# Graph message passing: one adding scatter for three steps, into a store that is zeroed ahead

## The chip, the cores and the metric

One core of one Trainium2 chip runs the whole kernel in one launch. The metric is the device time of the launch in microseconds (us); lower is better. The core has a matrix engine (PE; its weight loads are listed as PEld), a vector engine (DVE), a scalar engine (ACT), a general engine (POOL, which here issues the indirect transfers) and SyncE (SP, which here issues plain transfers). Each runs its own list of instructions in order; semaphores hold an instruction until others are done.

## The reference

```python
# N = 12500 nodes, E = 800000 edges, D = 64, 16 edge features
def reference(x, e_attr, src, dst, w_msg, w_upd):
    m_in = jnp.concatenate([x[src], x[dst], e_attr], axis=-1)
    msg = _silu(m_in @ w_msg)                          # one message of 64 an edge
    agg = _segment_sum(msg, dst, N)                    # summed at its target node
    return _silu(jnp.concatenate([x, agg], axis=-1) @ w_upd)
```

All is float32; `src` and `dst` are drawn at random.

## The kernel before

**Buckets.** The nodes are cut into 128 buckets of 98. An edge belongs to the bucket of its target. The kernel sorts the edges' records (16 features and one number that holds the source and the place in the bucket, 17 floats, `R`) by bucket into a store `st` in DRAM. Each bucket owns a stretch of it, and a pointer (`ptr`) says where its next record goes. At the same time it takes full tiles of 128 records of one bucket from the store and computes the messages and their sums.

**Steps.** The edges come as 6250 tiles of 128, in 782 *steps* of 8 tiles (`M`). A step runs through three periods: `onehot` and `sums` (ACT and DVE: which edge is in which bucket, and running counts); `count`, `ranks` and `expand` (PE sums give each edge its rank within its bucket in this *chunk*, and DVE writes its record into the slot of that rank, array `X`); `move` (PE multiplies the one-hot `hf` with `X` and so gathers, for each of 128 buckets, a row of slots in the PSUM tile `pl`). A chunk is several tiles whose products add up in one `pl`. The slots grow with the tiles (`LIM`: 13 for the first two tiles, then 17, 21, 24, 27, 30), so later tiles of a chunk have wider products. The first 140 chunks (`N8`) are *plain* ones of 8 tiles, one a step; then come 428 of 12 tiles (`C`), two in three steps. Such a triple of steps has three turns: turn 0 holds tiles 0 to 7 of its first chunk, turn 1 the last four of the first and the first four of the second, turn 2 tiles 4 to 11 of the second.

At a chunk's end ACT copies `pl` to `blk`, `Chunk.place` (DVE) makes the next pointer from the counts, and `Chunk.scatter` (POOL) writes the 128 rows to the store at the pointers that held before this chunk. A row is written with all its slots; the unused ones behind a bucket's end are overwritten by the next chunk. A chunk in which a bucket's slots do not suffice is noted in `LOST` and done again at the end.

**Groups and batches.** The kernel forms a *group* of 48, 24 or 64 tiles of the store (units of one, two, then four tiles) as soon as a plan made with random draws (`Draws`) is sure that they are full. SP loads them (`rt<-st`), and they are worked off in *batches* of 8 tiles (6 in the second kind): POOL gathers the sources' rows, one indirect transfer a tile (`g<-A_d`, L649); PE transposes (`tq`, L668) and multiplies (`pre`, L677), DVE adds, ACT applies silu, and PE sums per node (`ag`, L698), which DVE adds to `ACC` (L710). The gathers go into four buffers in turn; the first gather of a batch waits for the sum of the batch four before.

**Order.** `period()` writes the order out by hand: the new batch's first four gathers, then the scatter of the chunk that ended in the period before, then the other gathers; `onehot`; the group's small operations; `count`; the transposes; the sum `ag`; `ranks`; the message; `sums` and `expand`; `move`; `product`; and `place`. Each engine's list follows it. The steps end after 785 periods; periods with batches alone follow, then the last tiles of each bucket and the update of the nodes.

Of the kernel before, what the change touches and what calls it, by code (L numbers as in the profile page):

```python
# [24 lines left out]
N8 = 140  # L25
# [4 lines left out]
XR = 2 + W  # L30
# [14 lines left out]
SUMMED = "the sum that this reads waits for the gathers into its buffer, the older ones there were read ahead of them"  # L45
LISTED = "the work list holds buckets and tiles of the store"


def mpnn_kernel(tc, x, e_attr, src, dst, w_msg, w_upd, out):
# [7 lines left out]
    CAPT = (K8 * S8 + (NCH - K8) * S) // P + 2  # L57
# [3 lines left out]
    NREC = TOP * P  # L61
# [11 lines left out]
    with es:  # L73
# [11 lines left out]
        A_d = dr.tile([NB * BK, D], F32, name="A_d")  # L85
        XU_d = dr.tile([BK, NBK * D], F32, name="XU_d")
        st = dr.tile([NREC, R], F32, name="st")
        st_t = st.rearrange("(t e) c -> t (e c)", e=P)

# [34 lines left out]
        ioS = cb[:, BK:BK + S]  # L124
        hit = cb[:, P:P + M * S].rearrange("p (k s) -> p k s", s=S)
# [3 lines left out]
        nc.vector.tensor_scalar(out=ioS, in0=iof[:, 0:S], scalar1=RK, scalar2=None, op0=OP.add)  # L129

# [8 lines left out]
        nc.vector.tensor_scalar(out=ub[1], in0=ipf, scalar1=float(CAPT), scalar2=None, op0=OP.mult)  # L139
# [5 lines left out]
        capm = cp.tile([NBK, 2 + len(FIRST)], F32, name="capm")  # L145
# [191 lines left out]
        ACCf = ACC.rearrange("p b k -> p (b k)")  # L337
        for t in X:
            nc.gpsimd.memset(t[:, :, 0:1], 1.0)
        nc.gpsimd.memset(sent, 0.0)  # L340
# [6 lines left out]
        def later():  # L347
# [5 lines left out]
            if len(zeros) == 15:  # L353
                for k in range(P // SR):
                    nc.sync.dma_start(st_t[D0:D0 + DUM, k * SR * R:(k + 1) * SR * R], sent[0:DUM].rearrange("p a b -> p (a b)"))
            elif len(zeros) == 13:
                nc.sync.dma_start(BW[BK:KQ], w_msg[2 * D:2 * D + DE, None, :].to_broadcast([DE, NBK, D]))
# [4 lines left out]
        bp = pool("bp", 2)  # L362
# [8 lines left out]
        state = dict(x=0, rt=0, u=1, ptr=ptr0, done=done0, stage=0, taken=0, straight=True)  # L371

        blocks = []
        gathers = []
# [4 lines left out]
        class Step:  # L379


            def __init__(c, hi, rec, index, n=M):

                c.hi, c.rec, c.n = hi, rec, n
# [4 lines left out]

                c.last = {k: K8 + (index * M + k) // c.size for k in range(n) if c.pos[k] == c.size - 1}  # L390
# [44 lines left out]
            def expand(c, rs=None):  # L435
# [6 lines left out]
                nc.vector.tensor_tensor(out=c.x[:, :, 1], in0=rank, in1=limc[:, c.turn, :], op=OP.is_ge)  # L442
                nc.vector.tensor_tensor(out=hit, in0=ioS[:, None, :].to_broadcast([P, M, S]), in1=rank[:, :, None].to_broadcast([P, M, S]), op=OP.is_equal)
                for k in range(0, c.n, 2):
                    n = LIM[c.pos[k]]
                    nc.vector.tensor_tensor(out=c.x[:, k:k + 2, 2:2 + n * R].rearrange("p k (s c) -> p k s c", c=R), in0=hit[:, k:k + 2, 0:n, None].to_broadcast([P, 2, n, R]),  # L446
                                            in1=c.rec[:, k:k + 2, None, :].to_broadcast([P, 2, n, R]), op=OP.mult)

            def move(c, part=None):
# [4 lines left out]
                for k in reversed(range(c.n)) if whole else range(c.n):  # L454
# [6 lines left out]
                    w = 2 + LIM[n] * R  # L461
                    ends = n == (0 if whole else c.size - 1)
                    nc.tensor.matmul(pl[:, 0:w], c.hf[:, k, :], c.x[:, k, 0:w], start=(n == (c.size - 1 if whole else 0)), stop=ends, skip_group_check=True)  # L463
                    if ends:
                        w = 2 + LIM[c.size - 1] * R
                        end = Chunk(*c.last.values())
                        end.blk = bp.tile([NBK, XR], F32, name="blk")[:, 0:w]
                        nc.scalar.activation(end.blk, pl[:, 0:w], AF.Copy)  # L468
                return end

        class Chunk:


            def __init__(c, index):
                c.index, c.m = index, M if index < K8 else min(C, NT - K8 * M - (index - K8) * C)

            def place(c, ptr_new):

                c.ptr, b = state["ptr"], c.blk
                lost = LOST[:, c.index:c.index + 1]  # L480
                nc.vector.scalar_tensor_tensor(out=lost, in0=b[:, 1:2], scalar=0.0, in1=b[:, 0:1], op0=OP.is_gt, op1=OP.mult)
                nc.vector.scalar_tensor_tensor(out=ptr_new, in0=b[:, 0:1], scalar=lost, in1=c.ptr, op0=OP.subtract, op1=OP.add)
                state["ptr"] = ptr_new

            def scatter(c):
                i = nc.gpsimd.indirect_dma_start(out=st, out_offset=bass.IndirectOffsetOnAxis(ap=c.ptr, axis=0), in_=c.blk[:, 2:], in_offset=None)  # L486
                tc.declare_no_dep(i.ins, group="units", reason=WHOLE)
                blocks.append(i.ins)
# [4 lines left out]
        class Group:  # L493


            def __init__(g, u, ptr, done_old, done_new, ceil, gt=GT, base=None, cap=None, bt=BT):
# [4 lines left out]
                g.quick = cap is not None  # L501
                g.nl = NL[u]
# [32 lines left out]
            def fourth(g):  # L535
                k = g.k
                gu = g.gu
                if k == 0:
                    urec = g.u * P
                    c = (urec - 1) / (2.0 * urec) * (1.0 if g.ceil else -1.0)  # L540
# [8 lines left out]
                    nc.vector.scalar_tensor_tensor(out=new, in0=v, scalar=-MAGIC, in1=g.done_old, op0=OP.add, op1=OP.subtract)  # L549
                    nc.vector.tensor_tensor(out=t1, in0=g.base, in1=g.done_old, op=OP.add)  # L550
# [164 lines left out]
        def period(step=None, batch=None, ptr_new=None):  # L715
# [49 lines left out]
            if p:  # L765
                p.move(1)
            if e:
# [10 lines left out]
        class Draws:  # L778
# [21 lines left out]
            def free(d, u):  # L800
# [3 lines left out]
                return [[min((c - o * P) // r, k) - n for c, o, n, k in zip(*v, caps)] for v in zip(d.cnt, d.base, d.done)]  # L804
# [65 lines left out]
        def step():  # L870
# [5 lines left out]
            if pipe["z"] and pipe["z"].last:  # L876
# [310 lines left out]
```

## Time and profile before

| what | value |
|---|---|
| time, median of 3 runs | 10877.64 us (10877.01 to 10887.08) |
| span of the profiled execution | 10886.0 us (the longest of the three times is 10887.08) |
| busy: PE, DVE, POOL, ACT | 82%, 66%, 60%, 47% of the span |
| granted PE clock, mean | 0.885 |
| `g<-A_d` gathers on POOL | 6322, 949 ns each |
| `st<-blk` scatters on POOL | 568, about 1000 ns each |
| HBM read, written | 330.05 MB, 152.30 MB |

Line numbers (L649) are those of the kernel before. In a row of a timeline the first number is the start in us, the second the duration, then engine, line, operation, what it writes and reads (`out<-in`), and in brackets how long the engine was idle before it and what ended that. In a table of groups the busy time and the mean duration in ns of one follow the count, and then the idle time before them with its releasers ("issue": nothing that the profile shows; "remote": a semaphore whose release is matched to no instruction).

### The profile page before, as it was taken

How to read it: one execution, taken by the hardware profiler on the slowest of the kernel's cores; microseconds unless marked ns; L12 is line 12 of the kernel's file. 1: busy time of each engine (PE TensorE's matmuls, PEld its weight loads, DVE VectorE, ACT ScalarE, POOL GpSimd, SP SyncE). 2: the span in 40 equal slices, each digit the busy share in tenths (PEclk: the TensorE clock that was granted, in tenths of full speed). 3: DMA queues.
4: the chain of work that ended last, by engine and by line, in shares of the span. 5: the costliest groups of instructions: out<-in, count | busy, mean ns of one | idle time of the engine just before them, and what ended most of it. 6: DMA issues, size and time to landing. Idle time of an engine off the chain costs nothing. (4 is left out here: it accounts for less than half of the span.)

```text
span 10886.0 us, 155616 instructions
## 1 busy us (share of the span) xinstructions
PE 8949.9 (82%) x49053; PEld 6219.2 (57%) x49816; DVE 7231.4 (66%) x15936; ACT 5082.6 (47%) x12594; POOL 6571.4 (60%) x6908
## 2 busy tenths in 40 slices
PE   8788888888888888888888888888888888888556
PEld 5566655555555555555555555555555555555555
DVE  7777776666666666766666666666666666766232
ACT  6455554444444444444444444444444444544211
POOL 2565666666666666666666666666666666666555
PEclk9999998999989988999998999999899998988555
DMA  3111111111111111111111111111111111111212
GB/s 97 44 49 48 49 49 46 43 47 42 47 42 46 45 44 45 44 43 44 46 43 46 44 44 43 46 47 43 45 42 46 43 47 44 44 45 41 46 36 44
DMA packets 662903, 501.15 MB, mean 46 GB/s; under 512 B 492983, under 2 KB 529911, under 8 KB 662071
## 3 DMA queue, kind: packets, MB, share of 16 engines
q0 software_dynamic: 238976, 349.72, 12.3%
q1 hardware_dynamic: 422775, 141.27, 5.9%
q8 instruction: 400, 6.55, 0.3%
q14 instruction: 432, 3.54, 0.1%
q10 hardware_dynamic: 320, 0.07, 0.0%
HBM read 330.05 MB, written 152.30 MB: 44 GB/s over the span
## 5 line engine op out<-in xcount | busy, mean ns | idle before, releaser
L649 POOL DMA_INDIRECT g<-A_d,sidx x6322 | 5997.6, 949 | 3658.7 <-issue 1620.7
L463 PE MATMUL pl<-X,hf 128*128 128x291 f32 (+5 forms) x12512 | 4745.0, 524 | 476.4 <-issue 428.3
L463 PEld LDWEIGHTS pl<-X,hf 128*128 128x128 f32 x12512 | 2538.7, 211 | 2159.4 <-issue 1737.4
L446 DVE TENSOR_TENSOR X<-cb,rec 128x442 f32<-128x442 f32 (+5 forms) x3128 | 2646.6, 908 | 26.7
L396 ACT ACTIVATE hf<-iof,shi 128x128 f32<-128x128 f32 x6256 | 1908.8, 389 | 1360.4 <-PE pl L463 449.0
L671 ACT ACTIVATE qt<-tq 114x1024 f32<-114x1024 f32 (+1 forms) x818 | 811.7, 992 | 2951.3 <-remote 2298.5
L433 DVE TENSOR_REDUCE rank<-z 128x8 f32<-128x1024 f32 x782 | 954.5, 1221 | 1270.3 <-remote 874.9
L677 PEld LDWEIGHTS pre<-w,qt 114*128 114x128 f32 x10496 | 1392.5, 209 | 687.8 <-ACT qt L671 467.1
L677 PE MATMUL pre<-w,qt 114*128 114x64 f32 x10496 | 1395.2, 291 | 345.6 <-ACT qt L671 317.6
L710 DVE TENSOR_TENSOR ACC<-ag,ACC 64x98 f32 x1938 | 496.7, 256 | 1553.3 <-remote 1131.7
L698 PE MATMUL ag<-q,g 128*64 128x98 f32 x12644 | 882.3, 276 | 490.4 <-remote 236.2
L698 PEld LDWEIGHTS ag<-q,g 128*64 128x64 f32 x12644 | 681.6, 151 | 668.8 <-issue 381.7
L668 PE MATMUL tq<-ident,q 128*114 128x128 f32 x6322 | 929.9, 294 | 103.3 <-issue 91.5
L668 PEld LDWEIGHTS tq<-ident,q 128*114 128x114 f32 x6322 | 812.6, 147 | 238.7 <-issue 122.6
L397 ACT ACTIVATE hf<-hf,ones 128x1024 f32<-128x1024 f32 x782 | 898.8, 1149 | 25.4
L486 POOL DMA_INDIRECT st<-blk,ptrs x567 | 567.2, 1000 | 561.4 <-ACT blk L468 272.2
L659 DVE TENSOR_TENSOR q<-cb,lo 128x784 f32<-128x784 f32 (+1 forms) x818 | 768.7, 940 | 96.1 <-PE ag L698 46.3
L468 ACT ACTIVATE blk<-pl 128x512 f32<-128x512 f32 (+1 forms) x568 | 324.9, 572 | 818.2 <-PE pl L463 500.9
L426 PE MATMUL z<-G,onesb 128*128 128x384 bf16 x1564 | 529.8, 339 | 78.9 <-issue 25.2
L682 ACT ACTIVATE g<-g 128x512 f32<-128x512 f32 (+1 forms) x818 | 498.4, 609 | 192.5 <-DVE g L681 111.8
L681 DVE TENSOR_TENSOR g<-pre,g 128x512 f32<-128x512 f32 (+1 forms) x818 | 541.3, 662 | 51.4 <-issue 37.2
L677 PE MATMUL pre<-BW,qt 114*128 (+1 forms) x2148 | 326.3, 314 | 99.0 <-ACT qt L671 64.8
(138 smaller groups left out, 5243.9 us busy)
## 6 DMA issues: line engine op xcount, KB each, us to landing
g<-A_d,sidx POOLq DMA_INDIRECT x6322
ea<-in_e_attr SPq DMA_DIRECT2D x260, 192.0 KB
rt<-st SPq DMA_DIRECT2D x1312, 34.0 KB
st<-blk,ptrs POOLq DMA_INDIRECT x567
rt<-st SPq DMA_DIRECT2D x434, 8.5 KB
nodes<-in_x SPq DMA_DIRECT2D x62, 98.0 KB
ACC<-rt SPq DMA_DIRECT2D x11, 544.0 KB
rt<-st SPq DMA_DIRECT2D x320, 17.0 KB
```

The source lines that it names most:

```text
L396: nc.scalar.activation(c.hf[:, k, :], iof, AF.Square, bias=c.hi[:, k:k + 1])
L397: nc.scalar.activation(c.hf, c.hf, AF.Relu, bias=ones, scale=-1.0)
L433: nc.vector.tensor_reduce(out=c.rank, in_=c.z, axis=AX.X, op=OP.max)
L446: nc.vector.tensor_tensor(out=c.x[:, k:k + 2, 2:2 + n * R].rearrange("p k (s c) -> p k s c", c=R), in0=hit[:, k:k + 2, 0:n, None].to_broad ...
L463: nc.tensor.matmul(pl[:, 0:w], c.hf[:, k, :], c.x[:, k, 0:w], start=(n == (c.size - 1 if whole else 0)), stop=ends, skip_group_check=True)
L486: i = nc.gpsimd.indirect_dma_start(out=st, out_offset=bass.IndirectOffsetOnAxis(ap=c.ptr, axis=0), in_=c.blk[:, 2:], in_offset=None)
L649: j = nc.gpsimd.indirect_dma_start(out=t.g[:, i, :], out_offset=None, in_=A_d, in_offset=bass.IndirectOffsetOnAxis(ap=t.grp.sidx[:, k:k + ...
L659: nc.vector.tensor_tensor(out=t.q[:, 0:n, 0:BK], in0=ioB[:, None, :].to_broadcast([P, n, BK]), in1=t.grp.lo[:, i0:i0 + n, None].to_broadca ...
L668: nc.tensor.transpose(t.tq[0:KQ, j * P:(j + 1) * P], t.q[:, j, :], ident)
L671: nc.scalar.activation(t.qt[:, 0:w], t.tq[0:KQ, 0:w], AF.Copy)
L677: nc.tensor.matmul(t.pre[:, i * D:(i + 1) * D], t.qt[:, i * P:(i + 1) * P], w, start=True, stop=True)
L698: o = nc.tensor.matmul(t.ag[t.half(v), v // 2 * BK:(v // 2 + 1) * BK], t.g[:, i, :], t.q[:, i, 0:BK], start=(k == 0), stop=(k == u - 1))
```

## The change

Two consecutive 12-tile chunks, that is three steps, now make one row of 60 slots (`ROW`) and one scatter. In the first chunk of the pair the ranks run downwards from slot 29, in the second upwards from slot 30, so that each bucket's records of both lie side by side around the middle. The row is written at the old pointer + the first chunk's count − 30. Since it then begins with unused slots over records that are there already, the scatter adds (`compute_op=OP.add`) instead of writing, and the store must hold zeros: 265 pieces of 128 × 60 records, copied by SP from a zero tensor `Z_d` in DRAM, four pieces ahead (`LEAD`). If either chunk of a pair has a bucket that overflows, that bucket's row goes to a place aside. `blk` becomes one buffer `BLK` with two halves, and the counts are copied apart (`cnt`). `place` runs once a pair and makes the pair's own address (`to`) as well as the next pointer. Groups formed from step 38 on may only take units that end 30 records below the pointer (`back`). The plain chunks at the beginning are 53 instead of 140, so there are 53 plain chunks and 243 pairs.

```diff
-N8 = 140
+N8 = 53
...
-XR = 2 + W
+XR = 2 + W + 2
+ROW = 2 * S
+LEAD = 4
...
+    REACH = [S8 * (i + 1) for i in range(K8)] + [S8 * K8 + ROW * (i + 1) for i in range(NPR)]
+    PIECES = [(r + S + ROW - 1) // ROW for r in REACH]
...
+        ioD = cp.tile([P, 2, S], F32, name="ioD")
+        nc.vector.tensor_scalar(out=ioD[:, 0, :], in0=iof[:, 0:S], scalar1=-1.0, scalar2=RK + S - 1, op0=OP.mult, op1=OP.add)
+        nc.vector.tensor_copy(ioD[:, 1, :], ioS)
...
+        BLK = lp.tile([NBK, 2, W], F32, name="BLK")
...
             if len(zeros) == 15:
+                nc.sync.dma_start(Z_d, z[:, 0:ROW * R])
+                nc.sync.dma_start(st[ASIDE:NREC, :].rearrange("(b r) c -> b (r c)", b=NBK), z[:, 0:ROW * R])
...
+        def fill():
+            a = (P - S + len(filled) * ROW) * R
+            z = nc.sync.dma_start(st_b[:, a:a + ROW * R], Z_d)
+            tc.declare_no_dep(z.ins, group="blocks", reason=AHEAD)
+            tc.add_to_no_dep_group("zeros", z.ins)
+            filled.append(z.ins)
...
             def expand(c, rs=None):
...
-                nc.vector.tensor_tensor(out=c.x[:, :, 1], in0=rank, in1=limc[:, c.turn, :], op=OP.is_ge)
+                for a, b in ((0, C - M), (C - M, M)) if turn else ((0, M),):
+                    f = 1 if c.right[a] else 3 + W
+                    nc.vector.tensor_tensor(out=c.x[:, a:b, f], in0=rank[:, a:b], in1=lim[:, a:b], op=OP.is_ge)
...
+                    h = 0 if c.right[k] else S - n
+                    a = 2 + h * R
...
             def move(c, part=None):
...
-                    w = 2 + LIM[n] * R
+                    w = LIM[n] * R
+                    a, b, o = (0, 2 + w, 0) if c.right[k] else (2 + W - w, 4 + W, 2)
...
+            def keep(c, pl, right):
+                if c.single or c.side == 0:
+                    prior["cnt"] = sm.tile([NBK, 8], F32, name="cnt")
...
+                if c.main:
+                    nc.scalar.activation(c.cnt[:, c.side, :], pl[:, f:f + 2], AF.Copy)
+                c.blk = BLK[:, c.side, 0:n]
+                nc.scalar.activation(c.blk, pl[:, a:a + n], AF.Copy)
...
             def place(c, ptr_new):
...
+                    both, at, whole, to = [c.all[:, k:k + 1] for k in range(4, 8)]
+                    n, lost = c.cnt[:, :, 0], c.cnt[:, :, 1]
+                    c.ptr = to.bitcast(I32)
+                    nc.vector.tensor_scalar(out=whole, in0=lost[:, 0:1], scalar1=lost[:, 1:2], scalar2=0.0, op0=OP.add, op1=OP.is_equal)
+                    nc.vector.tensor_scalar(out=at, in0=ptr, scalar1=n[:, 0:1], scalar2=aside[:, 1:2], op0=OP.add, op1=OP.add)
+                    nc.vector.scalar_tensor_tensor(out=c.ptr, in0=at, scalar=whole, in1=aside[:, 0:1], op0=OP.mult, op1=OP.add)
+                    nc.vector.tensor_tensor(out=both, in0=n[:, 0:1], in1=n[:, 1:2], op=OP.add)
+                    nc.vector.scalar_tensor_tensor(out=ptr_new, in0=both, scalar=whole, in1=ptr, op0=OP.mult, op1=OP.add)
+                    nc.vector.scalar_tensor_tensor(out=LOST[:, i - 1:i + 1], in0=n, scalar=whole, in1=n, op0=OP.mult, op1=OP.subtract)
...
             def scatter(c):
...
+                if c.single:
+                    i = nc.gpsimd.indirect_dma_start(out=st, out_offset=at, in_=c.blk, in_offset=None)
+                else:
+                    i = nc.gpsimd.indirect_dma_start(out=st, out_offset=at, in_=BLK.rearrange("p a w -> p (a w)"), in_offset=None, compute_op=OP.add)
                 tc.declare_no_dep(i.ins, group="units", reason=WHOLE)
+                tc.declare_no_dep(i.ins, group="zeros", keep=filled[PIECES[n - 1] if n else 0:PIECES[n]], reason=AHEAD)
...
-                    c = (urec - 1) / (2.0 * urec) * (1.0 if g.ceil else -1.0)
+                    c = (urec - 1) / (2.0 * urec) * (1.0 if g.ceil else -1.0) - g.back / urec
...
+            if e and not e.whole:
+                e = None
             if e:
                 e.place(ptr_new)
...
+            state["back"] = S if flow["ic"] >= K8 - 15 else 0
+            ahead = min(flow["ic"], K8) + max(0, flow["ic"] - K8) * M // (2 * C)
+            while len(zeros) < 16 and len(filled) < min(PIECES[-1], PIECES[min(ahead, len(PIECES) - 1)] + LEAD):
+                fill()
```

100 lines of the change are left out of this document (66 added, 34 removed).

## The prediction

> **What bounds the kernel now.** I read the page first (engines, the costliest groups), then the busy time by stage, then the rows of POOL, DVE and ACT over four periods in the middle. A *period* is one call of `period()`: at most one step (8 edge tiles, into buckets) and one batch (6 or 8 tiles gathered from the store and summed).
>
> ```profile
> PE 8949.9 (82%) x49053; PEld 6219.2 (57%) x49816; DVE 7231.4 (66%) x15936; ACT 5082.6 (47%) x12594; POOL 6571.4 (60%) x6908
> HBM read 330.05 MB, written 152.30 MB: 44 GB/s over the span
> ...
> 60.00:160.00 100.00, 95.09 (x382) 61.70 (x390) 90.25 (x193) 81.15 (x216) 15.07 (x16) 0.98 0.43 130
> 600.00:1000.00 400.00, 329.89 (x1852) 241.96 (x1888) 304.90 (x801) 209.52 (x515) 239.55 (x250) 0.92 0.19 49
> 2000.00:9800.00 7800.00, 6574.45 (x35966) 4460.82 (x36549) 5351.82 (x11288) 3760.75 (x9380) 4839.48 (x5082) 0.91 0.17 45
> 10150.00:10800.00 650.00, 394.54 (x2351) 344.38 (x2350) 176.21 (x465) 118.82 (x235) 385.99 (x410) 0.56 0.23 40
> ```
>
> The columns after the window are busy time of PE, PEld, DVE, ACT and POOL, then granted clock, DMA share and GB/s. PE's 82% looks like the bound. But from 60 to 160 us, where steps run without batches, PE is 95% busy; from 2000 to 9800 us it is 84%, so there it has time left. The counts of `rank` (one a period with a step) and of the gathers give the periods' lengths:
>
> ```profile
> 60.00:160.00 100.00, 18.35 (x15) 0.98 0.43 130
> 600.00:1000.00 400.00, 43.82 (x36) 0.92 0.19 49
> 2000.00:9800.00 7800.00, 715.54 (x586) 0.91 0.17 45
> ...
> 10150.00:10800.00 650.00, 385.83 (x409) 0.56 0.23 40
> ```
>
> The first three rows are those of `rank`: 6.7 us without a batch, 11.1 us with plain steps and six-tile batches, 13.3 us with 12-tile chunks and eight-tile batches. The last is that of the gathers, after the steps have ended: 409 / 8 = 51 batches in 650 us, 12.7 us each, although PE has only 61% of work there and no step. What both stages share is POOL:
>
> ```profile
> 5010.81 0.95 POOL L649 DMA_INDIRECT g<-A_d,sidx  x1 [2.44 <-remote]
> 5012.06 0.94 POOL L649 DMA_INDIRECT g<-A_d,sidx  x1 [0.30 <-issue]
> ...
> 5015.81 1.00 POOL L486 DMA_INDIRECT st<-blk,ptrs  x1 [0.31 <-issue]
> ...
> 5020.88 0.94 POOL L649 DMA_INDIRECT g<-A_d,sidx  x1 [0.30 <-issue]
> 5024.34 0.95 POOL L649 DMA_INDIRECT g<-A_d,sidx  x1 [2.52 <-DVE g L681]
> ...
> 5028.10 0.94 POOL L649 DMA_INDIRECT g<-A_d,sidx  x1 [0.30 <-DMA g<-A_d,sidx]
> 5029.35 1.00 POOL L486 DMA_INDIRECT st<-blk,ptrs  x1 [0.30 <-issue]
> ...
> 5037.83 0.95 POOL L649 DMA_INDIRECT g<-A_d,sidx  x1 [2.48 <-remote]
> ...
> 5049.95 0.95 POOL L649 DMA_INDIRECT g<-A_d,sidx  x1 [2.39 <-remote]
> 10302.66 0.95 POOL L649 DMA_INDIRECT g<-A_d,sidx  x1 [2.33 <-PE ag L698]
> ```
>
> POOL issues its transfers back to back (about 0.95 us and 0.30 us of gap), and only the first gather of a batch waits, 2.4 us each time, with steps or without (last row). That gather waits for the sum `ag` that frees its buffer, and the sum is released about that long after POOL's last issue. So a period lasts as long as POOL's list plus 2.4 us. From start to start: 13.53 and 13.49 us with a scatter in the list, 12.12 us without. A scatter costs **1.4 us** of period.
>
> The Trainium skill (Perfetto Trace Analysis, Identifying the Most-Contended Engine) says that matmul busy time is a poor measure of PE's distance from its limit and that the other engines are to be ranked by occupancy. By that rule DVE (66%) stands above POOL (60%), and a shorter POOL list would bring nothing; the starts above disagree.
>
> **The change part by part.**
>
> *Scatters.* 568 become 53 + 243 = 296. The 782 steps run as 53 plain ones and 243 triples; 29 triples replace plain steps (53 to 139, beside six-tile batches), 214 replace triples that had two scatters. In a triple of the second kind the scatter of its first chunk goes: −1.4.
>
> *The pair's scatter waits for its pointer.* Today `scatter` uses the pointer as it stood before this chunk; `place` only makes the next one. Now the row starts at old pointer + left count − 30, or aside, so it needs three operations of this very `place` (`whole`, `at`, `to`), which stands on DVE behind the expansion of X. The period that places a right chunk, in DVE's rows:
>
> ```profile
> 5024.10 0.53 DVE L710 TENSOR_TENSOR ACC<-ag,ACC 64x98 f32 x2
> ...
> 5026.46 3.01 DVE L446 TENSOR_TENSOR X<-cb,rec 128x442 f32<-128x442 f32 x4
> 5029.39 0.15 DVE L481 SCALAR_TENSOR_TENSOR LOST<-blk 128x1 f32<-128x1 f32 x1
> 5029.57 0.22 DVE L482 SCALAR_TENSOR_TENSOR ptrs<-blk,LOST,ptrs 128x1 int32<-128x1 f32 x1
> 5027.23 0.60 ACT L468 ACTIVATE blk<-pl 128x512 f32<-128x512 f32 x1 [1.62 <-PE pl L463]
> ```
>
> `place` starts at 5029.39. The two ops of today start 0.18 apart, so three end at about 5030.0; with about 0.25 us more until POOL starts (its own gaps are 0.30) the scatter begins at 5030.25. Its turn on POOL, behind four gathers, was 5029.35. So it stands 0.9 us, and the four gathers queued behind it, the sum that waits for them and the next batch stand with it. Both ends start at the same event (`ag` ending near 5024.1 starts DVE's row and POOL's 5024.34), so the distance is fixed. I take +0.95 a triple; the ends are 0 (DVE early) and 1.9 (twice that).
>
> *The adding transfer on POOL.* No row shows one. Nearest is the plain scatter, 1.00 us for 128 rows of 2040 bytes; the gather takes 0.95 for rows of 256 bytes, so length costs nearly nothing. Below: no difference, or −0.05 as for a gather. Above: a second issue, 1.00 + 0.30. An add also has to read the old row, three sides where a copy has two; half as much again would be +0.5. I take half of that, **+0.25**, near the plain row.
>
> The Trainium skill (DMA: Bandwidth & Descriptors, Anatomy of one DMA) holds that many descriptors can be emitted before their generation shows. By that the term is 0 and the sum below 61 us lower, about no change; no run here shows an add.
>
> *PE loses its lead.* In triples the second period shrinks by 1.4, and the widest step (tiles 4 to 11 of a chunk) is multiplied there. PE needs 84% of 13.3 = 11.2 us a period. Where it is late the block's eviction is late, and the scatter with it:
>
> ```profile
> L486 POOL DMA_INDIRECT st<-blk,ptrs x100 | 100.1, 1001 | 72.0 <-ACT blk L468 34.3 <-issue 32.6 <-DVE LOST L481 3.9
> ```
>
> This is the group from 4000 to 6000 us: 0.34 us a scatter already goes to waiting for the block. I add as much again, +0.35 (ends 0, and the whole 1.4). The second eviction (two columns of counts) lies on ACT, 47% busy, behind `pre`'s matmuls, and costs nothing; without that cover it would add its own length to the block's wait. The extra DVE operations (six in place of four a triple, one more `is_ge`) run after the pointer or beside ACT's and PE's work: nothing, or three times 0.15 us a triple if DVE became the bound.
>
> Sum over 214 triples: −1.4 + 0.95 + 0.25 + 0.35 = +0.15 each, **+32 us**.
>
> *87 steps become wider.* From 4000 to 6000 us the six widths of `pl`:
>
> ```profile
> L463 PE MATMUL pl<-X,hf 128*128 128x512 f32 x400 | 192.3, 598 | 7.5 <-issue 6.6
> L463 PE MATMUL pl<-X,hf 128*128 128x461 f32 x400 | 192.1, 591 | 17.1 <-issue 15.3 <-DVE slo L148 1.1
> L463 PE MATMUL pl<-X,hf 128*128 128x359 f32 x400 | 185.6, 582 | 29.8 <-issue 26.5 <-DVE g L681 2.0 <-DVE rank L433 1.0
> L463 PE MATMUL pl<-X,hf 128*128 128x410 f32 x400 | 174.6, 555 | 18.6 <-issue 18.4
> L463 PE MATMUL pl<-X,hf 128*128 128x291 f32 x400 | 147.2, 479 | 30.3 <-issue 30.0
> L463 PE MATMUL pl<-X,hf 128*128 128x223 f32 x400 | 117.9, 417 | 14.4 <-issue 14.4
> ```
>
> Busy time by 400, two matmuls a tile: 0.84 us a tile over six widths, 0.78 over the four narrow ones: +0.5 us a step. By columns it would be 376 for 321, +17% of 6.25, +1.1. PE's 82% of 11.1 = 9.2 us rises to 9.7 to 10.3. POOL's side of a triple: two scatters fewer, −2.8, the one left +0.95 + 0.25, so −1.6, to 10.6 us a period. At the 95% that PE reached once it needs 10.2 to 10.8. I take −0.5 a triple, **−15 us** for 29 (ends −1.6 and +1.5: −46 and +44).
>
> *The groups lag.* From step 38 a group may only take tiles that lie 30 records below the pointer, and records count a pair at a time. Working the planner's rule through with its own random numbers: by the end of the loop of 785 periods 5832 tiles have been batched before, 5792 after; five batches move behind it (852 periods in all for 847). Each adds 12.7 us there and frees 13.3 − (6.7 + 0.5) = 6.1 us here: **+33 us** (ends −3 and +64: a freed period brings its whole 13.3 us, or nothing).
>
> *Zeros.* 265 pieces of 522 KB, DRAM to DRAM, on SP, four ahead of need. With the old rows read by the adds, traffic rises from 482 MB by 277 + 127 MB, and the DMA share of 0.17 to about 0.31: engines not full, a gather that meets a piece lands later. Estimate +10 (0 to 40). SP waits for each piece before the next tile load; those are used more than a period later. At the start the first scatters wait for Z_d and five pieces beside the tables' loads (DMA share 0.43): +6 (0 to 30).
>
> Together: 32 − 15 + 33 + 16 = **+66 us**. The profiled execution has a span of 10886.0 us, 1.1 below the longest run, 10887.1; the median of the three is 10877.6. 10886 + 66 = 10952 on that execution, 10944 on the median.
>
> **The rivals.**
>
> *The pointer comes in time.* If DVE reaches `place` 0.9 us earlier against POOL than in the rows above, nothing stands on POOL. For: evictions are often early (5027.23 + 0.60 against a turn at 5029.35). Against: the order on DVE is unchanged. It decides from a `place` that starts 0.65 us before the scatter's turn. With an add as dear as a copy and PE as assumed: 214 × (−1.4 + 0.35) = −225, 29 × −1.6 = −46 (as much as PE leaves there), +33 + 16: **10656** on the median. With half of the wait left, about 10760.
>
> *PE paces after all.* For: 82%, and the clock of 0.91. Then no scatter brings anything, 87 steps cost 0.5 to 1.1: +44 to +96, +33, +16: about **11000**. Against: batches without steps take 12.7 us. This is what the skill's ranking by occupancy comes to.
>
> *The add costs a second issue.* 1.05 more for 243: +255, **11199**. From an add of about 1.0 us longer than a copy the change is clearly a loss whatever the other terms do.
>
> **How the numbers follow.** My forecast's own range is 10870 to 11030, chance 0.42; the pointer in time, or half so, 0.28; PE 0.12; the dear add 0.18. Two tenths of a per cent (22 us) is about what a measurement can tell here, for the runs before differ by 10 us. Faster: 0.28 and a twelfth of 0.42, 0.31. Same: a quarter of 0.42 and a little of PE's, 0.12. Slower: 0.57. The range for eight in ten runs from the half-hidden wait, 10740, to just under the dear add, 11150.
>
> **What would show it.** Right: the pair's scatter has idle time ahead of it, released by DVE's pointer, near 1 us; two of three batch starts lie 12.1 to 12.3 us apart, the third 14.5 to 15; five more batches behind the last `rank`. The add's row gives its price at once. Wrong: starts at 12.1 with no wait (faster), equal starts with PE at 95% (PE's case), or a long gap ahead of gathers behind the add, if its landing, which the sum also waits for, is slow.

## The result and the profile after

The changed kernel takes 10994.92 us (median of 4, 10976.19 to 11010.07) where the kernel before takes 10882.36 (10877.01 to 10897.7) on the same chip: ratio **1.0099, 95% interval 1.0085 to 1.0114**, so slower by 113 us. Times differ from one set of runs to another (in later sets the kernel before takes 10728, 10732 and 10905), so below every kernel is compared by its ratio to the kernel before in its own set, or with a kernel of a set that is as fast.

The profiled execution has a span of 10993.9 us, 107.9 above that of before. Its page:

```profile
PE 9009.2 (82%) x49087; PEld 6245.5 (57%) x49845; DVE 7347.0 (67%) x16853; ACT 5091.6 (46%) x13088; POOL 6471.8 (59%) x6638
HBM read 468.45 MB, written 288.71 MB: 69 GB/s over the span
```

Busy shares have not moved by more than a point; the traffic has grown by 138 MB read and 136 written. The 265 pieces of zeros are 138 MB on either side, so the profile counts no read for the adds; the kernel with plain writes in their place, below, shows the same 468.45 MB. The 127 MB that the prediction added for the old rows stand in no figure here. The same four windows (busy time of PE, PEld, DVE, ACT and POOL, then granted clock, DMA share, GB/s):

```profile
60.00:160.00 100.00, 94.49 (x387) 61.75 (x393) 85.47 (x175) 78.98 (x223) 13.63 (x15) 0.98 0.65 186
600.00:1000.00 400.00, 343.42 (x1797) 231.77 (x1831) 325.36 (x840) 201.22 (x512) 214.81 (x216) 0.92 0.29 59
2000.00:9800.00 7800.00, 6569.85 (x35861) 4481.29 (x36443) 5378.48 (x11933) 3767.11 (x9759) 4762.37 (x4868) 0.89 0.28 57
10150.00:10800.00 650.00, 375.35 (x2217) 326.06 (x2218) 180.01 (x519) 117.46 (x237) 370.24 (x393) 0.56 0.22 37
```

The DMA share rises to 0.65 at the start and 0.28 in the main stage (0.31 was estimated). Where the 108 us lie is read from the starts of `rank`, of which there is one a step:

| stretch, between the `rank` of steps | before, us | after, us | difference |
|---|---|---|---|
| 0 to 20 | 151.0 | 168.8 | +17.8 |
| 20 to 53 | 382.0 | 383.3 | +1.3 |
| 53 to 140 (six-tile batches) | 970.0 | 987.0 | +17.0 |
| 140 to 781 | 8517.4 | 8497.6 | -19.8 |
| last step to the end | 849.2 | 940.7 | +91.5 |

The loop with its 782 steps costs 16 us, the batches behind it 91. Now POOL's groups (x count, busy us, mean ns of one, then idle time before them):

```profile
L725 POOL DMA_INDIRECT g<-A_d,sidx x6322 | 6018.1, 952 | 3465.3 <-issue 1720.5 <-PE ag L774 708.1 <-remote 563.5
L557 POOL DMA_INDIRECT st<-BLK,cnt x243 | 395.4, 1627 | 729.1 <-ACT hf L428 314.2 <-issue 251.5 <-ACT BLK L529 132.0
L555 POOL DMA_INDIRECT st<-BLK,ptr x1 | 1.1, 1146 | 37.8 <-DMA st<-Z_d 37.8
```

An adding scatter takes 1.63 us to issue, the plain one 1.00. Ahead of the 243 stand 729 us of idle time, 3.0 each; 0.30 of that is POOL's usual gap. The releasers named are not the true ones, as the next rows show. The third row is the very first scatter: it now waits for zeros and starts at 39.86 us, where it started at 33.07. A triple of the main stage on POOL, and the `place` in it on DVE:

```profile
5004.50 0.94 POOL L725 DMA_INDIRECT g<-A_d,sidx  x1 [3.24 <-PE pl L503]
...
5016.63 0.95 POOL L725 DMA_INDIRECT g<-A_d,sidx  x1 [2.44 <-remote]
...
5020.38 0.94 POOL L725 DMA_INDIRECT g<-A_d,sidx  x1 [0.30 <-issue]
5023.00 1.63 POOL L557 DMA_INDIRECT st<-BLK,cnt  x1 [1.67 <-issue]
5024.93 0.98 POOL L725 DMA_INDIRECT g<-A_d,sidx  x1 [0.30 <-issue]
...
5030.05 0.95 POOL L725 DMA_INDIRECT g<-A_d,sidx  x1 [0.30 <-issue]
...
5042.63 0.94 POOL L725 DMA_INDIRECT g<-A_d,sidx  x1 [2.88 <-remote]
```

```profile
5018.64 3.01 DVE L485 TENSOR_TENSOR X<-cb,rec 128x442 f32<-128x442 f32 x4
5021.57 0.20 DVE L543 TENSOR_SCALAR cnt<-cnt 128x1 f32<-128x1 f32 x1
5021.69 0.26 DVE L544 TENSOR_SCALAR cnt<-ptrs,cnt,capm 128x1 f32<-128x1 int32 x1
5021.99 0.22 DVE L545 SCALAR_TENSOR_TENSOR cnt<-cnt,capm 128x1 int32<-128x1 f32 x1
```

The pointer (L545) ends at 5022.21 and the scatter starts at 5023.00, 0.79 us later. Over the main stage that distance is 0.79 for every pair, from the 5th to the 95th percentile: it is the pointer that releases the scatter, whatever the group's row names. The stall beyond the gap is 1.37 here, 2.57 in the mean; it comes mostly (136 of 190) as 1.4, 2.6 or 3.9, in steps of one gather (1.25).

The batch starts stand 12.1, 13.4 and 12.6 us apart here (5004.50, 5016.63, 5030.05, 5042.63). In the mean of the main stage the stretch with the scatter is 14.6 and each of the others 12.5, where the prediction's sign of being right was 14.5 to 15 and 12.1 to 12.3. The batch behind the scatter, at 5030.05, does not wait at all: 0.30. Over the main stage, leaving out the stretches around a few long waits that come below, the terms of a triple are:

| term, us a triple | before | after | difference | predicted |
|---|---|---|---|---|
| 24 gathers, and the gaps ahead of 21 of them | 29.25 | 29.25 | 0 | 0 |
| scatters with their gaps | 2 x 1.30 | 1.93 | -0.67 | -1.15 |
| stalls ahead of scatters | 0.87 | 2.57 | +1.70 | +1.30 |
| idle ahead of the three batches | 7.1 | 5.9 | -1.25 | 0 |
| from start to start | 39.83 | 39.60 | -0.23 | +0.15 |

One thing is not in the prediction at all. Ten batches of the main stage start after 10 to 17 us of idle time; before, the longest such wait was 8.0, once. The first of them on POOL, and on DVE:

```profile
1801.69 0.95 POOL L725 DMA_INDIRECT g<-A_d,sidx  x1 [0.31 <-issue]
1813.08 0.95 POOL L725 DMA_INDIRECT g<-A_d,sidx  x1 [10.44 <-issue]
```

```profile
1808.25 3.96 DVE L485 TENSOR_TENSOR X<-cb,rec 128x714 f32<-128x714 f32 x4
1812.13 0.21 DVE L604 CAST sidx<-rt 128x64 int32<-128x64 f32 x1
```

`sidx`, the gathers' list of rows, is cast once a group by `fifth`, the last thing in DVE's list of a period. POOL stands at the next period's first gather from 1802.94 on, and the cast ends at 1812.34; the gather follows 0.74 us later. Following the planner's rule through, this is a group whose first batch comes in the fifth period after the one that formed it, the earliest that `ready` allows; the cast stands at the end of the fourth. Of 80 groups of the last kind in the changed kernel's loop, eight begin so, and they wait 10.4 to 17.5 us; the other 72 wait 0.3 to 3.4. Before it was one of 81 (the 8.0). Two of the ten long waits are something else, a catching-up: four batches behind a gap, where POOL has run ahead without waits. The six-tile stage has one late group too, which waits 10.4 us at 578 us; the kernel before has none there.

### The profile page after: what moved, and what is told of

Same layout as the page of the kernel before. It is cut to its first block, busy times and chain, and to the rows that moved or that the text cites. A ratio compares the mean times of both kernels' runs of the same rounds, so it can differ in the third digit from the quotient of the medians.

```text
span 10993.9 us, 157490 instructions
## 1 busy us (share of the span) xinstructions
PE 9009.2 (82%) x49087; PEld 6245.5 (57%) x49845; DVE 7347.0 (67%) x16853; ACT 5091.6 (46%) x13088; POOL 6471.8 (59%) x6638
## 3 DMA queue, kind: packets, MB, share of 16 engines
HBM read 468.45 MB, written 288.71 MB: 69 GB/s over the span
## 5 line engine op out<-in xcount | busy, mean ns | idle before, releaser
L503 PE MATMUL pl<-X,hf 128*128 128x410 f32 (+5 forms) x12512 | 4701.3, 525 | 265.4 <-issue 246.8
L485 DVE TENSOR_TENSOR X<-cb,rec 128x442 f32<-128x442 f32 (+5 forms) x3128 | 2688.1, 922 | 27.0
L774 PE MATMUL ag<-q,g 128*64 128x98 f32 x12644 | 973.9, 274 | 621.0 <-issue 528.8
L774 PEld LDWEIGHTS ag<-q,g 128*64 128x64 f32 x12644 | 715.3, 149 | 855.9 <-issue 739.0
L557 POOL DMA_INDIRECT st<-BLK,cnt x243 | 395.4, 1627 | 729.1 <-ACT hf L428 314.2
L527 ACT ACTIVATE cnt<-pl 128x2 f32<-128x2 f32 x539 | 91.2, 169 | 980.1 <-PE pl L503 525.0
L753 PE MATMUL pre<-BW,qt 114*128 (+1 forms) x2276 | 352.7, 319 | 124.6 <-ACT qt L747 72.7
```

The lines of the kernel that those rows point to most:

```text
L485: nc.vector.tensor_tensor(out=c.x[:, k:k + 2, a:a + n * R].rearrange("p k (s c) -> p k s c", c=R), in0=hit[:, k:k + 2, h:h + n, None].to_b ...
L503: nc.tensor.matmul(pl[:, a - o:b - o], c.hf[:, k, :], c.x[:, k, a:b], start=(n == (c.size - 1 if whole else 0)), stop=ends, skip_group_che ...
L753: nc.tensor.matmul(t.pre[:, i * D:(i + 1) * D], t.qt[:, i * P:(i + 1) * P], w, start=True, stop=True)
L774: o = nc.tensor.matmul(t.ag[t.half(v), v // 2 * BK:(v // 2 + 1) * BK], t.g[:, i, :], t.q[:, i, 0:BK], start=(k == 0), stop=(k == u - 1))
```

## The experiments

Four theories were in play. *Pointer*: the pair's scatter waits for its own `place`, in the middle of the batch's gathers, and that eats what a scatter fewer gives. *Add*: the adding transfer is dear in itself. *PE*: PE paces the triple, so nothing on POOL counts. *Edges*: the loss lies in the start, the wide early steps, the zeros and the batches moved behind the loop. The runs come in three sets. In the first (the late scatter, the plain writes, the 140 plain chunks in the changed kernel, the doubled matmul) the kernel before takes 10728 us; in the second (the same move in the kernel before, no zeros, the 53 plain chunks, the late scatter with 140) 10905; in the third (the changed kernel again, the zeros twice, the zeros one piece ahead, the groups that lag more) 10732.

**The scatter behind all eight gathers.**

```diff
             if q:
-                q.gather(0, BT // 2)
+                q.gather(0, BT)
             if s:
                 s.scatter()
-            if q:
-                q.gather(BT // 2, BT)
```

> The changed kernel with the scatter behind all eight gathers of the batch instead of between the fourth and the fifth. Theory A (POOL's list paces; the pair's scatter stands 2.7 us on average waiting for its address, and the gathers behind it with it): five microseconds later the address is there, the wait goes, a triple falls from 40.05 to about 24 x 1.25 + 1.9 + 3 x 2.4 = 39.1 us, the whole to 10995 - 0.95 x 214 - 30 = about 10760. Theory B (PE paces, the wait lies in time that POOL had over): 10995 within 20.

Measured: 10568.25 us, ratio 0.9851 (0.9828 to 0.9874): faster than both kernels, by 1.5% and 2.5%. The rows of POOL, and the group:

```profile
5026.62 0.95 POOL L725 DMA_INDIRECT g<-A_d,sidx  x1 [2.33 <-remote]
...
5035.36 0.94 POOL L725 DMA_INDIRECT g<-A_d,sidx  x1 [0.30 <-issue]
5036.61 1.63 POOL L557 DMA_INDIRECT st<-BLK,cnt  x1 [0.30 <-issue]
5039.99 0.98 POOL L725 DMA_INDIRECT g<-A_d,sidx  x1 [1.75 <-remote]
```

```profile
L557 POOL DMA_INDIRECT st<-BLK,cnt x243 | 395.5, 1627 | 130.8 <-issue 76.8 <-ACT BLK L529 21.3 <-DVE LOST L548 12.3
```

The add costs the same 1.63, the stall is gone (729 us of idle time to 131, of which 73 are the gaps), and the triple without the long waits is 37.79 us, against 38.94 for the changed kernel in a set as fast. 1.15 x 214 = 246 us of the 267 between them. That is theory A with a larger gain (its 10760 us would be 0.989). On POOL the triple loses 2.2 us of stall and gets 1.1 back as longer waits ahead of its batches (5.6 to 6.7). Less the 0.6% that the same move brings the kernel before (next), 1.9% is left, so the pointer's wait costs more than the whole loss. Two things move with it and are not parted from it: the granted clock rises from 0.87 to 0.90, and the first gather behind the add lands after 2.64 us instead of 3.85.

**The same move in the kernel before.**

```diff
-                q.gather(0, BT // 2)
+                q.gather(0, BT)
...
-            if q:
-                q.gather(BT // 2, BT)
```

> The kernel before with one edit: each scatter stands behind all eight gathers of its period, not behind four. It asks how much of the 1.5% between the kernel before and the changed kernel with the late scatter comes from the place alone. Theory A (the place only takes away stalls, and the kernel before has few): in the main stage the kernel before lost 0.44 us a scatter beyond the 0.30 us gap, 428 scatters, 188 us; part of it is given back by the next batch's first gather, so -60 to -190 us, 10540 to 10670 where before takes 10730, ratio 0.982 to 0.994; triple of periods 39.0 to 39.6 us. Theory B (a scatter between the gathers costs more than its stall, whatever it waits for, for the gathers behind it land late): the gain is that of the changed kernel, 2.5% (0.975), triple 38.5 us or less. Theory C (in the kernel before the stalls are hidden by the wait for the sum): within 20 us, triple 39.8 to 40.0 us.

Measured: 10840.18 us where before takes 10904.54, ratio 0.9940 (0.9927 to 0.9954). That is the low end of theory A; the stall goes to 0.006 us a scatter:

```profile
L486 POOL DMA_INDIRECT st<-blk,ptrs x567 | 566.8, 1000 | 348.1 <-issue 161.6 <-ACT nodes L196 99.5 <-ACT blk L468 58.2
```

Where the scatter stands is worth 0.6% to the kernel before and 2.5% to the changed one. So 0.985 against 0.994 is what pairing brings once the wait is out of the way: nearly 1%, or 0.65% by the late kernel with 140 plain chunks (0.9875, below), which ran in the same set as this one. The granted clock rises here too, from 0.88 to 0.90.

**Plain writes in place of adds.**

```diff
-                    i = nc.gpsimd.indirect_dma_start(out=st, ..., compute_op=OP.add)
+                    i = nc.gpsimd.indirect_dma_start(out=st, ...)
```

> The changed kernel with a plain write in place of the add (later rows then overwrite records of earlier ones with zeros, so values are lost; counts, addresses and all other work stay). The add's issue took 1.63 us, the plain one 1.00. Theory A: 0.63 x 243 = 150 us less, 10845. Theory B, or a wait that only becomes longer elsewhere: 10995 within 20. If the adds' reads of DRAM slow the gathers' landings, another 10 to 40 less.

Measured: 11066.99 us, ratio 1.0312 (1.0285 to 1.0339), slower than with adds, and neither theory's time.

```profile
L557 POOL DMA_INDIRECT st<-BLK,cnt x243 | 242.5, 998 | 829.8 <-ACT hf L428 377.9 <-issue 276.7 <-ACT BLK L529 138.9
```

The issue falls from 1.63 to 1.00 as the add's price would have it, but the stall grows, from 2.25 us (the changed kernel in a set as fast) to 3.07, and the gathers land 3.1 us after their start, not 2.1. With the lost records many gathers read one and the same row; whether that or the write slows them was not separated. The add's price is therefore taken from its row, 0.63 us, and this run's time proves nothing on it.

**Plain writes and no zeros.** As the last one, and:

```diff
-            while len(zeros) < 16 and len(filled) < min(PIECES[-1], PIECES[min(ahead, len(PIECES) - 1)] + LEAD):
-                fill()
```

> The changed kernel with plain writes in place of adds and without the 265 pieces of zeros: rows overwrite records that lie there and unwritten rows hold no zeros, so part of the records is lost; its time is read only against the other kernel with plain writes, which had the zeros (ratio to before 1.0312). Theory A (the prediction's 16 us, and the 18 us that the first 20 steps lost): 15 to 40 us less, ratio 1.027 to 1.030, the first 20 steps back at about 150 us, the triple unchanged at 40.7 us. Theory B (the zeros' traffic, 277 MB, delays the gathers in the main stage too): 0.3 to 1 us a triple less, 70 to 230 us in all, ratio 1.010 to 1.024.

Measured: 11065.68 us where before takes 10904.54, ratio 1.0156 (1.0141 to 1.0172). By the ratios that is theory B, 1.6% for the zeros. But the absolute time is the same as with zeros, in a set where the kernel before is 1.6% slower, and the triples are 40.32 with zeros and 40.12 us without. In both kernels the gathers land late for a cause that was not separated, and I do not trust the comparison between two sets here; the run with the zeros doubled, below, is the better test. One thing carries over: the first 20 steps take 157.0 us, so of the 17.8 us lost there some 12 are the zeros'.

**The zeros twice.**

```diff
+        Y_d = [dr.tile([NBK, ROW * R], F32, name=f"Y{i}") for i in range(16)]
...
             z = nc.sync.dma_start(st_b[:, a:a + ROW * R], Z_d)
+            nc.sync.dma_start(Y_d[len(filled) % 16], Z_d)
```

> The changed kernel, but each of the 265 pieces of zeros is also copied a second time, into scratch memory that nobody reads: 277 MB written and read more, 265 more transfers on SP. It prices the zeros by doubling them. Theory A (the prediction's +16 us, and the 18 us of the first 20 steps): +10 to +40 us against the changed kernel, most of it in the first 53 steps. Theory B (the comparison of the two kernels with plain writes, with and without zeros, stands for the zeros' traffic: 1.5%): +100 to +200 us, 0.4 to 0.9 us a triple. Theory C (hidden): within 10 us, also at the start.

 

For it, the next run and the last one, the changed kernel itself was run in the same set:

> The changed kernel as it is, to stand beside the next three on one chip. Every theory: ratio to before 1.007 to 1.013, triple 39.9 us where before takes 39.9 us, 2.5 to 2.7 us of stall ahead of a pair's scatter.

Measured: the changed kernel 10835.01 us (1.0095, 1.0078 to 1.0112), with the zeros doubled 10863.68 (1.0121, 1.0104 to 1.0137). So 277 MB more written and read cost 29 us: by the profiled executions 10.6 in the first 20 steps and 0.1 us a triple. That is theory A's size but not its place, for most of it lies behind step 140; B, which the last run suggested, does not hold.

**Zeros one piece ahead, with the late scatter.**

```diff
-LEAD = 4
+LEAD = 1
```

> The changed kernel with the scatter behind all eight gathers and with the zeros only one piece ahead instead of four, so that four pieces go ahead of the first scatter where seven did. Theory A (the first 20 steps lose their 15 to 18 us to the pieces' traffic beside the tables' loads): 5 to 10 us less than the late kernel there, ratio to before 0.983 to 0.986. Theory B (they lose it to the first scatter's wait for the zero tensor itself): within 3 us of it there, 0.984 to 0.987. Theory C (one piece ahead is too little, scatters wait for zeros in the main stage): a stall ahead of the scatter of over 0.5 us, ratio above 0.99.

Measured: 10574.04 us, 0.9853 (0.9836 to 0.9869), no different from the late kernel. The first 20 steps take 161.7 us against 166.1, nearly theory A's 5, and the time at the end does not show it.

**53 plain chunks in the kernel before**, and nothing else.

```diff
-N8 = 140
+N8 = 53
```

> The kernel before with 53 plain chunks instead of 140 and nothing else: 29 triples with two scatters each take the place of 87 plain steps with three, beside six-tile batches. Theory A (the prediction's: PE is near its limit there, a wider step costs 0.5 to 1.1 us more of it): 87 x 0.5 to 1.1 = +44 to +96 us between steps 53 and 140, less up to 29 x 1.4 = 41 us of scatters, so 0 to +60 there, and one batch more behind the loop, +7 to +13; ratio 1.001 to 1.007. Theory B (POOL's list sets the six-tile periods too): 29 x -1.4 = -41 us there, +10 behind: ratio 0.996 to 0.998. If the first step of the pairs (from 53 on) and not the pairs themselves made the 17 us between steps 53 and 140 of the changed kernel, this one shows at least +17 there.

Measured: 10924.86 us, ratio 1.0019 (1.0009 to 1.0028): +20 us. Between steps 53 and 140 it takes 959.7 us, 10 less than the profiled execution of before, and behind the last step 884.2, 35 more. That stretch lies between the theories (0 to +60 and -41): 29 scatters fewer should give 41 us by the prediction's 1.4, so the wide steps can hide up to about 30, 0.35 a step, where PE's work says 0.5 to 1.1; or a scatter gives less there. The loss is behind the loop, where the plan now leaves 64 tiles more to be taken in units of one.

**140 plain chunks with the pairs**, in the changed kernel as it is, and then with the late scatter.

```diff
-N8 = 53
+N8 = 140
```

> The changed kernel with 140 plain chunks again (214 pairs). The stage of six-tile batches gets its narrow steps and its plain scatters back. Both theories: that stage 17 us shorter; one period with a batch alone less at the end (851 for 852), and 64 tiles there in larger units: together about 35 less, 10960. If the pairs were a gain beside six-tile batches, the time would rise instead.

Measured: 10829.05 us, 1.0088 (1.0059 to 1.0117). The stretch from 53 to 140 takes 956.4 us, where the changed kernel in a set as fast takes 976.3, and the total is the same, not 35 us less: the stretch from 140 to 781 takes 26 us more, with 12 late groups instead of eight.

> The changed kernel with the scatter behind all eight gathers and with 140 plain chunks instead of 53. Theory A (with the scatter late the pairs cost the same beside six-tile batches as plain steps do): one batch less behind the loop and the plain steps' 956 us between steps 53 and 140 against 959, so -3 to -20 us against the late kernel with 53: ratio to before 0.983 to 0.985. Theory B (58 scatters fewer in that stage are worth 1.3 us each once they do not wait): +40 to +75 us against it, ratio 0.989 to 0.992.

Measured: 10769.08 us where before takes 10904.54, 0.9875 (0.9859 to 0.989), a quarter of a per cent worse than with 53, between the two theories. Again 12 groups start late. With the scatter late and 53 chunks the stretch from 53 to 140 takes 958.9, 17 less than in the changed kernel (976.3), so the pointer's wait alone is worth the 17 us that the change lost there. It is no faster than plain steps (956.4), though it has 58 scatters fewer: what these should give goes elsewhere, to the one late group, to the wide steps or to both.

**Is PE the pace?** In the kernel before, the first of the two matmuls of every `count` is issued twice.

```diff
+                    nc.tensor.matmul(c.z[:, k:k + ZB, :], w1, hb[:, k:k + ZB, :], start=True, stop=True)
```

> The kernel before with the first matmul of each half of the counts done twice (its first result is overwritten): two more matmuls of 512 bf16 columns a step, 0.24 to 0.41 us each, 0.5 to 0.8 us of PE a step, in all 782 steps. Theory A (PE has time over beside batches): no more than 10 to 40 us, from the first 25 steps, which run at PE's pace, and the six-tile stage: 10890 to 10925. Theory B (PE paces): 390 to 620 us more, 11270 to 11500.

Measured: 10859.22 us, ratio 1.0122 (1.01 to 1.0144): +131 us. Neither theory: too much for a PE that is covered, far too little for one that paces. What was added is read from the rows of PE, from the start of the added matmul (L425) to that of the one behind it (L426):

```profile
4948.99 0.40 PE L425 MATMUL z<-hf,w 128*128 128x512 bf16 x1
4949.23 0.39 PE L426 MATMUL z<-hf,w 128*128 128x512 bf16 x1
```

The 1564 added matmuls take 0.25 us of PE each in the mean, 387 us in all, so about a third of what is added shows. (PE's busy time is only 242 us more than in the profiled execution of before, but that profile lacks 763 records of this very matmul.) PE is near enough to the path that its lead counts, as the prediction had it, and POOL's order weighs more: the late scatter takes 2.5% with the same work on PE. It ran at a clock of 0.90 instead of 0.87; but the kernel with the doubled matmul has 0.90 too, and is 1.2% slower.

**Groups that lag more.** The changed kernel with groups that may only take units ending 150 records below the pointer (30 in the change).

```diff
-            state["back"] = S if flow["ic"] >= K8 - 15 else 0
+            state["back"] = 5 * S if flow["ic"] >= K8 - 15 else 0
```

> The changed kernel, but groups formed from step 38 on may only take units that end 150 records below the pointer instead of 30. The plan then has 870 periods instead of 852: 18 batches more behind the loop. It prices a batch that is moved behind the loop. Theory A (the prediction's: it costs 12.7 us behind and frees 6.1 us in the loop): 18 x 6.6 = +119 us against the changed kernel, 90 to 150. Theory B (the period that loses its batch gives back all of its 13.3 us): -10 to +20 us. Theory C (nothing is given back in the loop, and the groups that form late make further waits): +200 to +290 us. If A, the five batches of the change are 33 us of its 112; if C, 60 to 90.

Measured: 10851.1 us (1.0121, 1.0103 to 1.0138) against 10835.01 for the changed kernel in this set: +16 us for 18 batches moved, theory B by the total. By stretches: 185.5 us more behind the loop (10.3 a batch), 190 less in it. But the loop's gain is not the freed periods alone. The waits of POOL in the main stage (total us, times, longest), first the changed kernel in this set, then this one:

```profile
POOL g L725 <- issue: 1273.1, 4061, 12.1
...
POOL g L725 <- PE ag L774: 364.9, 127, 17.2
```

```profile
POOL g L725 <- issue: 1259.3, 4130, 0.3
...
POOL g L725 <- PE ag L774: 324.5, 122, 3.9
```

The waits of 12 and 17 us are gone: by the planner's rule groups now start eight to fourteen periods after they were formed, because the plan runs out of tiles early, skips batches there and then has a lead. (Ahead of the window shown, between 500 and 2000 us, four batches still wait 7 to 27 us for their cast.) Counting all batches, three intervals take 39.46 us in the changed kernel and 38.89 here; without the stretches around the long waits 38.94 and 38.88. So the long waits were worth some 100 us over the main stage, and by subtraction the 18 freed periods gave the rest, about 5 us each.

## Why the prediction was right, and where not

The direction held, and the sum (+66 against +113) lies 47 us short. It named the right mechanism: POOL's list sets the period, the pair's scatter stands for its pointer in the midst of the gathers, and this takes away what a scatter fewer gives. Moving only the scatter turned a loss of 1% into a gain of 1.5%. That the sum came out near is in part luck: hardly a term has its size, and the 214 triples, which were to cost 32 us, save some 49. The terms:

- **Pointer in time: no.** Each pair waits. But the stall was mis-sized: 2.57 us where I had 0.95 and 0.35 for PE's lead. From the pointer to the scatter's start pass 0.79 us, where I took 0.25 from POOL's gap between transfers that wait for nobody; and `place` starts later against POOL's turn than in the one row of before that I read. That row (5029.39 against 5029.35) is the earliest case and the commonest, but not the mean. Here is another right chunk of the kernel before:

```profile
5987.13 1.00 POOL L486 DMA_INDIRECT st<-blk,ptrs  x1 [0.30 <-issue]
5988.44 0.20 DVE L481 SCALAR_TENSOR_TENSOR LOST<-blk 128x1 f32<-128x1 f32 x1
```

Of its 190 right chunks in the main stage 113 have their `place` at the turn, the others one to three gathers later, 0.94 us in the mean; in the changed kernel it is 1.06. So 0.94, three operations of 0.64 together and 0.79 would have given 2.37 from the profile of before and that one latency. I had called the distance fixed. It is not: it jumps by whole gathers, in both kernels. Why it takes these steps was not found.
- **The add**: +0.63 us, where I took +0.25 between ends of -0.05 and 1.05. Half as much again as a copy (the +0.5 that I halved) was nearer. It doesn't come to a second issue. By the Trainium skill (DMA: Bandwidth & Descriptors, Anatomy of one DMA) many descriptors can be emitted before it shows, and the prediction drew a price of 0 from that. Here 128 rows cost 0.63 us more to issue as an add, so that price does not hold; whether it is the number of descriptors that costs was not tested.
- **"A period lasts as long as POOL's list plus 2.4 us"** is the rule that failed, to the change's good. It holds while the sum waits for POOL. Behind a scatter that has stood for 2.6 us the sum of four batches ago is long done, and the batch starts after 0.30; about 0.6 of the 2.1 saved returns as longer waits ahead of the next one. Dearer stall, dearer add and this credit leave -0.23 a triple where the sum had +0.15: -49 us, not +32.
- **Wide early steps** (-15 predicted, +17 measured from 53 to 140): the stall again, against -1.6 counted, and one late group of 10.4 us; what the wider steps themselves cost is not parted from it, at most about 30 us by the kernel before with 53 plain chunks.
- **The groups lag** (+33): the price of a moved batch was about right, 10.3 us behind the loop less about 5 in it (the latter by subtraction), in place of 12.7 less 6.1. What it left out is that a plan without slack also starts groups late. The eight late groups and the gaps ahead of two of them lengthen their stretches (12 batches each) by about 34 us for six of them together and 35 and 21 for the others, against the median stretch of 159.4. And it took 12.7 us for each batch behind the loop where the stage grew by 91.5 for five; the kernel before with 53 plain chunks shows 35 of that with only one batch more.
- **Zeros and start** (+16): 17.8 us in the first 20 steps, and about 18 in the rest if the doubled zeros' price is taken for the first ones; twice what I had.

By stretch, then: +18 start, +1, +17 six-tile steps, -20 main stage (-49 for the triples; +90 for the eight stretches just named, less 39 for three batches fewer in them; -11 for the one long wait that the kernel before had there; some -10 that I can't assign), +91.5 behind. The predicted +0.15 a triple would have matched the mean over all triples (39.89 to 40.08), but that mean contains the late groups; as a sum of its own terms it was wrong in three places that offset each other.

Of the rivals: "PE paces after all" is out as the whole story and in as a share (131 us for 387 of added work), and DVE, which the ranking by occupancy in the Trainium skill (Perfetto Trace Analysis, Identifying the Most-Contended Engine) puts above POOL, was not the bound: moving one POOL instruction took 2.5% while DVE's busy time stayed at 7347 and 7369 us.

## What to carry to other kernels

When an edit makes an instruction depend on something computed in the same period, look first at what stands behind it in its queue; the cheapest repair is to move it behind them, and the move can be worth more than the edit. A wait found in a steady rhythm ("list plus 2.4 us") belongs to two parties: delay one and the other's wait vanishes, so price a stall net of the waits that it covers. A distance between two engines that is read from one period may be one of several that recur: take it over the whole stage before a stall is priced from it. And when work is planned ahead, the slack is part of the price: a plan that only just has its tiles ready loses periods, which no count of batches shows.

## What the runs showed of the hardware

- An indirect scatter that adds costs 1.63 us to issue for 128 rows of 4080 bytes, the same rows written plainly 1.00, as do plain rows of half the length. In the DMA records the add is 128 packets of 4080 bytes, 0.43 us each in the mean, the plain write 64 of 8160, 0.33 us each. The add lands 5.6 us after its start, and the three gathers queued right behind it after 3.85, 3.1 and 2.5 us instead of 2.1 (read from the DMA records of the changed kernel's main stage).
- From the end of the DVE instruction that makes the list of rows to the start of the transfer pass 0.79 us for the pair's pointer and 0.74 for a group's list, where transfers that wait for nobody follow each other after 0.30.
- The mean granted clock was 0.87 in the kernels with the pair's scatter in mid-batch and 0.90 in the late one, in sets where the kernel before takes the same time. It is 0.90 as well in the kernel before with the late scatter (0.6% faster) and with the doubled matmul (1.2% slower), so clock and time do not go together in these runs. Whether the clock follows the stalls or adds to them was not tested.
- Late placement can be had without the pairs and the pairs without early placement; the best kernel here is the changed one with its scatter behind all eight gathers, at 0.985. It still has the eight late groups, so forming those a period or two earlier should give more; that was not tried.
